# A two-layer expert kernel: the first expert's output product with weights stationary for the two-tile chunks

## The chip, the cores and the metric

The kernel runs on one core of a Trainium2 chip. The metric is the device time of one execution in microseconds (us). The core has a matrix engine (TensorE, PE in the profile; its loads of the stationary operand are the separate row PEld), a vector engine (DVE), an activation engine (ACT), GpSimd (POOL) and a queue that issues DMAs (SyncE, SP). Each engine executes its own instructions in the order in which the program lists them and waits on semaphores for the others. Matrix products accumulate in PSUM banks of 512 fp32 numbers for each of 128 partitions; ACT copies them to SBUF, from where DMAs go to DRAM.

## What is computed

Attention with a top-32 mask over 4 batches, 8 heads, 576 positions and head size 64; its output, as 2304 tokens of 512 numbers, goes through a gated expert (512 to 1536 to 512) and then through a second expert with a cosine (512 to 2048 to 512). All in fp32.

```python
scores = q @ k.T / 8
mask   = scores >= (32nd largest of the row)
attn   = softmax(where(mask, scores, -1e9))
x  = (attn @ v) as [2304, 512]
g  = x @ w_gate
x1 = (g * sigmoid(g) * (x @ w_val)) @ w_out      # first expert
h  = x1 @ w_in
out = (h * cos(h)) @ w2_out                      # second expert
```

## The kernel before

The 2304 tokens are 18 tiles of 128. They are worked on in ten chunks: two chunks of one tile (chunks 0 and 1, "turned" and in plain fp32) and eight chunks of two tiles, 256 tokens (chunks 2 to 9). In the two-tile chunks each fp32 operand is split into a high and a low fp32r part, and a product is three matmuls: high with high, low with high, high with low.

A chunk goes through these stages. Attention: for each of 4 head pairs, each tile and each head a "unit" (144 in all): scores on PE (`unit_proc`, line 586 plain in chunks 0 to 2, line 593 in split parts later), a copy by ACT (line 598), four maxima and three strikes on DVE (lines 623 and 626), the exponential on ACT, transposes of the result (line 687), the product with v (lines 740 and 743), and the normalised output x (the last step is line 824 on POOL). First expert: for each of 12 slices f of the hidden size the gate and value products (`gemm_proc`, line 899; gv, in the last chunk gvl), the activation, and a high and a low part gh and gl of the result (lines 958 and 962); then the output product (`wout_proc`, line 1063), accumulated over the 12 slices in two PSUM banks y0 and y1. The slice's weights wo (512 KB, high and low) come by DMA into a ring of two buffers. Second expert: `h_proc` (line 1279) and `o_proc` (line 1344); its input is read back from DRAM, transposed, as [feature, token] (`x2_proc`).

In `wout_proc` a two-tile chunk has the tokens as stationary operand: for each slice and each of the two tiles three matmuls with a 128x128 block of gh or gl stationary and 512 columns of wo moving (line 1063). So bank y0 holds 128 tokens x 512 features, y1 the next 128 tokens. The second expert wants features on the partitions, so `y_proc` turns each bank: for each half of it a copy to SBUF by ACT (line 1096, tile yo), two transposes on PE back into the bank (line 1102), a second copy by ACT (line 1107) and a DMA to DRAM (line 1108). There is one yo buffer (`r_yo`, a ring of 1), so a half starts when the DMA of the half ahead of it is done. A bank is free for the next chunk (`r_y`) after its second half.

The order of the instructions is made ahead of time, in Python, by `Plan`: every step is a generator that yields an engine, an estimated cost, a function that issues the instructions, and a due time. `Plan.run` picks, of the steps that are ready by these estimates on the engine that is free first, the one that is due earliest. The chip then executes the lists as they are. Each step of an output product is due 5 us after the gate and value product of the same slice (`moe_due`), and these are spread evenly over the time of one chunk's attention. A change of one cost can therefore change the order anywhere behind it.

Of the kernel before, what the change touches and what calls it, by code (L numbers as in the profile page):

```python
# [9 lines left out]
F32 = mybir.dt.float32  # L10
# [6 lines left out]
AF = mybir.ActivationFunctionType  # L17
# [36 lines left out]
RAWC = 3  # L54
SC_LEAD = 14.0
# [106 lines left out]
def topk_attention_moe_moe(ctx: ExitStack, tc: tile.TileContext, qT, kT, vP, w1, wo1, w2, out):  # L162
    nc = tc.nc
    plan = Plan()
# [3 lines left out]
    y1 = dram.tile([128, KT, NTOK], F32, name="y1")  # L168
# [12 lines left out]
    pools = {}  # L181

    def opened(name, **kw):
        pools[name] = tc.alloc_tile_pool(name=name, bufs=1, **kw)
        return pools[name]

    moe = opened("moe")
# [5 lines left out]
    psG = opened("psG", space=PSUM)  # L193
    gvt = [psG.tile([128, DM], F32, name=f"gv{g}") for g in range(2)]
    yt = [psL.tile([128, DM], F32, tag=f"y{i}", name=f"y{i}") for i in range(NYB)]
    sc = psR.tile([128, 2, 512], F32, name="sc")

    nc.scalar.activation(halfpi, halfpi, AF.Copy)
# [21 lines left out]
    r_pre, r_wo = Ring(6), Ring(2)  # L220
# [27 lines left out]
    W1X, W1, WO = {}, {}, {}  # L248
# [4 lines left out]
    ev_wo = {(c, f): Event() for c in range(NCH) for f in range(NF1)}  # L253
# [53 lines left out]
    def wo_index(c, f):  # L307
        return c * NF1 + f
# [247 lines left out]
    r_x, r_rs = Ring(NX), Ring(1)  # L556
# [9 lines left out]
    def unit_proc(u):  # L566
        c, p, t, h = units[u]
        segs = segments(FIRST[c] + t)
        due = due_unit(u)
        st = {}  # L570
        g = group[c, t]
        t0, n = ATT[c][g]
# [25 lines left out]
            nc.scalar.activation(st["s"], sc[:, :, :HALF], AF.Copy)  # L598

        yield r_sc.gate(u)  # L600
        end = yield "PE", 0.575 * len(segs) if c >= RAWC else 0.98, qk, due - SC_LEAD, True
        if h and (c, t) == (RAWC - 1, SIZES[c] - 1):
            r_k.free(1 + p, end, plan)
        for b, r0, r1 in segs:
# [4 lines left out]
        end = yield "ACT", 0.53, copy, due - SC_LEAD + 1.0, True  # L609
# [9 lines left out]
        for i in range(TOPK // 8):  # L619
# [9 lines left out]
            end = yield "DVE", 0.675, best, due, True  # L629
# [9 lines left out]
        end = yield "POOL", 0.175, bounds, due, True  # L639
# [16 lines left out]
        end = yield "ACT", 0.68, keep, due + 6.0, True  # L656
# [11 lines left out]
        end = yield "ACT", 0.77, expo, due + 9.0, True  # L668
# [173 lines left out]
    NG0 = KT // 2  # L842
    G0 = [sum((NF1 // 2 - NG0) // 2 if turned else NF1 for turned in TURNED[:c]) for c in range(NCH)]
    for i in range(G0[PLAIN]):
        r_g.freed[i] = Event(2)
    GV0 = [sum(NF1 // 4 if turned else NF1 for turned in TURNED[:c]) for c in range(NCH)]
    ev_y1 = [Event() for _ in range(NTOK // 128)]
    yo_count = [0]

    def moe_due(c, f):  # L850
        return due_unit((FIRST[c] + SIZES[c]) * H) + 20.0 + f * SIZES[c] * H * PACE / NF1
# [194 lines left out]
        for j in range(2):  # L1046
            ev_g[c, 2 * fp + j].set(end, plan)

    def wout_proc(c):
        turned = TURNED[c]  # L1050
        for f in range(NF1):
            k = c * NF1 + f
            yield ev_g[c, f]
            yield ev_wo[c, f]

            def part(t, f=f, k=k):
                bank = yt[(FIRST[c] + t) % NYB]
                cs = slice(t * 128, t * 128 + 128)
                g = G[c, f // 2][:, f % 2] if turned else None
                terms = ((g, WO[k]),) if turned else [(G[c, f][m][:, cs], WO[k][:, a])  # L1060
                                                      for m, a in ((0, 0), (1, 0), (0, 1))]
                for n, (m, w) in enumerate(terms):
                    nc.tensor.matmul(bank, m, w, start=f == 0 and n == 0, stop=f == NF1 - 1 and n == len(terms) - 1)  # L1063

            for t in range(SIZES[c]):
                i = FIRST[c] + t
                if f == 0:
                    yield r_y[i % NYB].gate(i // NYB)
                end = yield "PE", 0.93 if turned else 0.7, lambda t=t, part=part: part(t), moe_due(c, f) + 5.0, False
                if f == NF1 - 1:  # L1070
                    plan.start(y_proc(c, i), end)
            if not turned:
                r_g.free(G0[c] + f, end, plan)
            elif f % 2 and f // 2 >= NG0:
                r_g.free(G0[c] + (f // 2 - NG0) // 2, end, plan)
            if c:
                r_wo.free(wo_index(c, f), end, plan)
            else:
                wo0_free(f, end)
        if turned:  # L1080
            r_x.free(2 + c, end, plan)

    def y_proc(c, i):
        due = moe_due(c, NF1)
        bank = yt[i % NYB]
        y4 = bank.rearrange("p (f n) -> p f n", f=KT)
        for half in range(2):
            ko = yo_count[0]
            yo_count[0] += 1
            yield r_yo.gate(ko)  # L1090
            y2 = y4[:, 2 * half:2 * half + 2]
            st = {}

            def fetch(y2=y2):
                st["y"] = moe.tile([128, 2, 128], F32, tag="yo", name="yo", bufs=r_yo.n)
                nc.scalar.activation(st["y"], y2, AF.Copy)

            yield "ACT", 0.27, fetch, due, True

            def turn(y2=y2):  # L1100
                for j in range(2):
                    nc.tensor.transpose(y2[:, j], st["y"][:, j], ident)

            yield "PE", 0.22, turn, due + 2.0, True

            def store(y2=y2, half=half):
                nc.scalar.activation(st["y"], y2, AF.Copy)
                nc.sync.dma_start(y1[:, 2 * half:2 * half + 2, i * 128:i * 128 + 128], st["y"])

            end = yield "ACT", 0.27, store, due, True  # L1110
            r_yo.free(ko, end + 2.5, plan)
        r_y[i % NYB].free(i // NYB, end, plan)
        ev_y1[i].set(end + 2.5, plan)


    O_LAG = 12.0
# [1 line left out]
    ev_pb, ev_pbx, ev_ph, ev_pbo = Event(), Event(), Event(), Event()  # L1118
# [100 lines left out]
    def x2_proc(j):  # L1219
        yield ev_pb  # L1220
        pb = pools["pb"]
        for i in range(j * TPB, (j + 1) * TPB):
            yield ev_y1[i]
        due = b_due(j, 0) - (25.0 if j else 75.0)
        st = {}
        yield r_x2s.gate(j)

        def hi(k):
            if k == 0:
                X2[j] = [pb.tile([128, KT, CB], F32R, tag=f"x2{a}", name=f"x2{a}", bufs=r_x2s.n) for a in "hl"]  # L1230
            nc.scalar.activation(X2[j][0][:, k], st["x"], AF.Copy)  # L1231

        def load(k):
            st["x"] = pb.tile([128, CB], F32, tag="x2", name="x2", bufs=r_x2.n)
            nc.sync.dma_start(st["x"], y1[:, k, j * CB:j * CB + CB])

        for k in range(KT):
            yield r_x2.gate(j * KT + k)
            yield "DMA", 1.0, lambda k=k: load(k), due, True
            yield "ACT", 0.41, lambda k=k: hi(k), due, True  # L1240
            end = yield ("POOL", 0.95,
                         lambda k=k: nc.gpsimd.tensor_sub(X2[j][1][:, k], st["x"], X2[j][0][:, k]), due, True)  # L1242
            r_x2.free(j * KT + k, end, plan)
        ev_x2[j].set(end, plan)
# [3 lines left out]
    def h_proc(j, f):  # L1248
        k = j * NF2 + f
        due = b_due(j, f)  # L1250
# [4 lines left out]
        if k < H_ONE:  # L1255
            second, third, i = False, k % 3 == 2, k // 3 if k % 3 == 2 else k // 3 * 2 + k % 3
        else:
            second, third, i = k % 2, False, (k - H_ONE) // 2 if k % 2 else H_ONE * 2 // 3 + (k - H_ONE) // 2
        rh = r_hb if second else r_hc if third else r_h
        if second:  # L1260
            yield r_y[i % 2].gate(NTOK // 128 // NYB)
        elif not third:
            yield ev_ph
        yield rh.gate(i)
        pb = pools["pb"]
        st = {}
# [15 lines left out]
        for kk in range(KT):  # L1282
            end = yield "PE", 0.526, lambda kk=kk: part(kk), due, False
# [13 lines left out]
        def rest():  # L1297
# [5 lines left out]
        end = yield ("DVE", 0.46, lambda: nc.vector.scalar_tensor_tensor(r, st["k"], -C2, r, op0=OP.mult,  # L1303
                                                                        op1=OP.add), due, True)
# [10 lines left out]
        end = yield "DVE", 0.46, prod, due, True  # L1315
# [11 lines left out]
        end = yield "DVE", 0.46, lambda: nc.vector.tensor_sub(GT[j, f][1], st["g"], GT[j, f][0]), due, True  # L1327
# [64 lines left out]
    for c in range(NCH):  # L1392
        for f in range(NF1):
            if c:
                plan.start(wo_proc(c, f))
            if not TURNED[c]:
                plan.start(gemm_proc(c, f))
            elif f % 2:
                plan.start(turned_gemm_proc(c, f // 2))
        plan.start(wout_proc(c))  # L1400
    plan.start(pool_b_proc())
    plan.start(pool_h_proc())
    plan.start(pool_c_proc())
# [48 lines left out]
```

## Time and profile before

| | us |
|---|---|
| median of three runs | 1257.34 |
| lowest and highest of them | 1255.83, 1258.74 |
| the profiled execution | 1255.94 |
| its span, first to last instruction | 1253.9 |
| PE busy | 1200.3 |
| PEld busy | 1043.6 |
| DVE busy | 975.1 |
| ACT busy | 923.8 |
| POOL busy | 632.0 |

The span is the time from the first to the last instruction in one profiled execution; some 2 us lie around it. Attention and the first expert fill the span up to about 860 us, side by side; behind that there is the second expert alone. PE's busy time counts each matmul with its latency, and overlapping ones once, so the pace of matmuls is read from the starts of neighbours in a timeline, not from their durations.

### The profile page before, as it was taken

How to read it: one execution, taken by the hardware profiler on the slowest of the kernel's cores; microseconds unless marked ns; L12 is line 12 of the kernel's file. 1: busy time of each engine (PE TensorE's matmuls, PEld its weight loads, DVE VectorE, ACT ScalarE, POOL GpSimd, SP SyncE). 2: the span in 40 equal slices, each digit the busy share in tenths (PEclk: the TensorE clock that was granted, in tenths of full speed). 3: DMA queues.
4: the chain of work that ended last, by engine and by line, in shares of the span. 5: the costliest groups of instructions: out<-in, count | busy, mean ns of one | idle time of the engine just before them, and what ended most of it. 6: DMA issues, size and time to landing. Idle time of an engine off the chain costs nothing.

```text
span 1253.9 us, 22487 instructions
## 1 busy us (share of the span) xinstructions
PE 1200.3 (96%) x7528; PEld 1043.6 (83%) x7528; DVE 975.1 (78%) x1938; ACT 923.8 (74%) x2081; POOL 632.0 (50%) x1082
## 2 busy tenths in 40 slices
PE   6799889999999999999999999999999999999998
PEld 3577657898888898988898988897999989898997
DVE  6999999999999999998999993447555555555553
ACT  4789999899888888888898876557565656565554
POOL 4898976776777776877776755533010101010000
PEclk9799989999999999999999999999999999999999
DMA  7555556665656655556555332871010101010000
GB/s 253 159 175 168 179 163 201 206 211 168 194 164 180 190 170 175 181 162 203 181 160 189 124 116 85 268 261 39 1 51 1 51 1 51 1 38 1 18 8 26
DMA packets 88547, 162.14 MB, mean 129 GB/s; under 512 B 17008, under 2 KB 44144, under 8 KB 88432
## 3 DMA queue, kind: packets, MB, share of 16 engines
q1 hardware_dynamic: 88272, 160.65, 40.4%
q8 instruction: 59, 0.97, 0.3%
q14 instruction: 56, 0.46, 0.1%
q10 hardware_dynamic: 160, 0.07, 0.0%
HBM read 133.41 MB, written 27.26 MB: 128 GB/s over the span
## 4 chain that ended last, share of the span: by engine, by line
PE 58%; DMA 8%; ACT 6%; POOL 3%; DVE 2%; issue 2%; SPq 0%; POOLq 0%; ACTq 0%
PE o L1344 16%; PE h L1279 15%; PE gv L899 10%; PE y L1063 7%; PE av L743 2%; PE sc L593 2%; DMA wo<-wo 2%; DMA kx<-in_kT 2%; PE tp L687 2%; PE gvl L899 2%; DMA y<-yo 1%; DMA w_raw<-in_w 1%; DMA qx<-in_qT 1%; ACT e L654 1%; POOL K L496 1%
## 5 line engine op out<-in xcount | busy, mean ns | idle before, releaser
L623 DVE MAX8 m<-w 128x8 f32<-128x576 f32 x432 | 311.0, 747 | 1.8
L899 PE MATMUL gv<-x,w 128*128 128x256 f32 x2016 | 283.7, 288 | 1.7 <-ACT hg L866 1.6
L899 PEld LDWEIGHTS gv<-x,w 128*128 128x128 f32 x2016 | 259.0, 190 | 8.6 <-ACT hg L866 2.8
L1279 PE MATMUL h<-x2h,w 128*128 128x384 f32 x768 | 214.5, 338 | 0.0
L626 DVE MATCH_REPLACE8 w<-m,w 128x576 f32<-128x576 f32 x288 | 213.3, 742 | 0.0
L1344 PE MATMUL o<-w,gh 128*128 128x512 f32 x576 | 195.8, 395 | 0.0
L1242 POOL TENSOR_TENSOR x2l<-x,x2h 128x384 fp32r<-128x384 f32 x24 | 25.8, 1075 | 262.1 <-ACT x2h L1231 262.1
L1063 PE MATMUL y<-wo,gh 128*128 128x512 f32 x400 | 148.5, 413 | 6.7 <-DMA wo<-wo 5.1
L1313 DVE TENSOR_TENSOR g<-r,h 128x384 f32<-128x384 f32 x96 | 53.1, 554 | 118.5 <-ACT r L1308 118.5
L1279 PEld LDWEIGHTS h<-x2h,w 128*128 128x128 f32 x768 | 140.6, 188 | 4.3
L1279 PE MATMUL h<-x2l,w 128*128 128x384 f32 x384 | 129.3, 337 | 0.0
L1306 ACT ACTIVATE r<-r 128x384 f32<-128x384 f32 x96 | 50.4, 525 | 103.9 <-DVE r L1303 103.9
L1344 PEld LDWEIGHTS o<-w,gh 128*128 128x128 f32 x576 | 108.1, 188 | 21.0
L654 ACT ACTIVATE e<-s,b 128x576 f32<-128x576 f32 x144 | 114.2, 794 | 8.2 <-POOL b L637 8.1
L623 DVE MAX8 m<-s 128x8 f32<-128x576 f32 x144 | 107.7, 748 | 15.9 <-ACT s L598 14.5
L665 ACT ACTIVATE e<-e,b 128x576 f32<-128x576 f32 x144 | 114.2, 793 | 2.8 <-POOL b L641 0.3
L1344 PE MATMUL o<-w,gl 128*128 128x512 f32 x288 | 113.6, 394 | 1.0 <-DVE gl L1327 1.0
L598 ACT ACTIVATE s<-sc 128x576 f32<-128x576 f32 x144 | 95.4, 662 | 21.6 <-PE sc L586 16.2
L626 DVE MATCH_REPLACE8 w<-m,s 128x576 f32<-128x576 f32 x144 | 106.9, 742 | 0.0
L693 ACT ACTIVATE pt<-tp 128x512 f32<-128x512 f32 (+1 forms) x216 | 101.9, 503 | 4.9 <-PE tp L687 3.3
L687 PE MATMUL tp<-ident,e 128*128 128x128 f32 x648 | 99.4, 277 | 5.9 <-ACT pt L693 3.3
L1327 DVE TENSOR_TENSOR gl<-g,gh 128x384 fp32r<-128x384 f32 x96 | 56.4, 588 | 58.0 <-ACT gh L1324 58.0
(106 smaller groups left out, 2489.6 us busy)
## 6 DMA issues: line engine op xcount, KB each, us to landing
wo<-wo SPq DMA_DIRECT2D x96, 512.0 KB, 3.7
w_raw<-in_w SPq DMA_DIRECT2D x32, 511.8 KB, 4.3
V<-in_vP SPq DMA_DIRECT2D x52, 256.0 KB, 3.0
w<-in_w SPq DMA_DIRECT2D x24, 511.5 KB, 5.5
kx<-in_kT SPq DMA_DIRECT2D x64, 144.0 KB, 3.1
wo<-wo SPq DMA_DIRECT2D x36, 256.0 KB, 2.9
w2d<-w_raw SPq DMA_DIRECT2D x32, 256.0 KB, 2.6
cvx<-w2d SPq DMA_DIRECT2D x32, 256.0 KB, 4.5
```

The costliest lines, as they stand in the source:

```text
L598: nc.scalar.activation(st["s"], sc[:, :, :HALF], AF.Copy)
L623: nc.vector.max(out=st["m"][:, 8 * i:8 * i + 8], in_=st["w"] if i else st["s"])
L626: nc.vector.match_replace(out=st["w"], in_to_replace=st["m"][:, 8 * i:8 * i + 8], in_values=st["w"] if i else st["s"], imm_value=LOWEST)
L654: nc.scalar.activation(st["e"], st["s"], AF.Prelu, bias=st["b"][:, 1:2], scale=SCALE, alpha=STEEP)
L665: nc.scalar.activation(st["e"], st["e"], AF.Exp, bias=st["b"][:, 2:3], scale=1.0, accum_out=smT[c, p, g][:, j:j + 1])
L687: nc.tensor.transpose(st["ps"][:, j - j0], e[:, j * 128:j * 128 + 128], ident)
L693: nc.scalar.activation(pt[:, j0:j1], st["ps"][:, :j1 - j0], AF.Copy)
L899: nc.tensor.matmul(gv[g], W1[f, kk // 2][:, a, g, kk % 2], m, start=kk == 0 and i == 0, stop=kk == KT - 1 and i == 2)
L1063: nc.tensor.matmul(bank, m, w, start=f == 0 and n == 0, stop=f == NF1 - 1 and n == len(terms) - 1)
L1279: nc.tensor.matmul(st["h"], w[:, a, kk * 128:kk * 128 + 128], m[:, kk], start=kk == 0 and n == 0, stop=kk == KT - 1 and n == 2)
L1327: end = yield "DVE", 0.46, lambda: nc.vector.tensor_sub(GT[j, f][1], st["g"], GT[j, f][0]), due, True
L1344: nc.tensor.matmul(o[t], a[:, cs], W2[f, 1][:, m], start=f == 0 and n == 0, stop=f == NF2 - 1 and n == 2)
```

## The change

For the eight two-tile chunks the operands of the output product change places. For each slice and each of four blocks d of 128 features, three matmuls have a 128x128 block of wo stationary (high, high, low) and 256 tokens of gh, gl and gh moving: 12 matmuls of 256 columns for each slice, where there were 6 of 512. Bank y0 then holds feature blocks 0 and 1, y1 blocks 2 and 3, each with features on the partitions and 256 tokens along the row. So nothing is transposed: each of the four blocks is copied once by ACT and stored by DMA. The turned one-tile chunks keep the old way, in a function of their own.

The steps on PE are four for each slice, with an estimated cost of 0.38 each, instead of two with 0.7. Bank y0 is free after the copy of block 1, y1 after that of block 3; the product of the next chunk asks for y0 ahead of block 0 and for y1 ahead of block 2. The copies still go through the one yo buffer, but those of chunk 8 (`late`) wait until the attention's memory is given back and then use four buffers of their own. The events of stored tiles become events of stored chunks. In `unit_proc` the estimated cost of a unit's scores goes from 0.98 to 1.25 in the plain chunks, and from 0.575 to 0.58 for each segment in the others.

```diff
+    y1p = [x.rearrange("p (a b) -> p a b", a=2) for x in yt]
...
-        end = yield "PE", 0.575 * len(segs) if c >= RAWC else 0.98, qk, due - SC_LEAD, True
+        end = yield "PE", 0.58 * len(segs) if c >= RAWC else 1.25, qk, due - SC_LEAD, True
...
+    def bank_turn(c, b):
+        return c // 2 if c < PLAIN else c - PLAIN + (PLAIN + 1 - b) // 2
...
-                terms = ((g, WO[k]),) if turned else [(G[c, f][m][:, cs], WO[k][:, a])
-                                                      for m, a in ((0, 0), (1, 0), (0, 1))]
-                for n, (m, w) in enumerate(terms):
-                    nc.tensor.matmul(bank, m, w, start=f == 0 and n == 0, stop=f == NF1 - 1 and n == len(terms) - 1)
...
-                end = yield "PE", 0.93 if turned else 0.7, lambda t=t, part=part: part(t), moe_due(c, f) + 5.0, False
-                if f == NF1 - 1:
-                    plan.start(y_proc(c, i), end)
...
+    def wout_proc(c):
+        t0 = FIRST[c] * 128
+        for f in range(NF1):
+            k = c * NF1 + f
+            due = moe_due(c, f) + 5.0
+            yield ev_g[c, f]
+            yield ev_wo[c, f]
+
+            def part(d, f=f, k=k):
+                w = WO[k]
+                gh, gl = G[c, f]
+                for i, (a, m) in enumerate(((0, gh), (0, gl), (1, gh))):
+                    nc.tensor.matmul(y1p[d // 2][:, d % 2], w[:, a, d * 128:d * 128 + 128], m,
+                                     start=f == 0 and i == 0 and d % 2 == 0, stop=f == NF1 - 1 and i == 2,
+                                     skip_group_check=True)
+
+            for d in range(KT):
+                if f == 0 and d % 2 == 0:
+                    yield r_y[d // 2].gate(bank_turn(c, d // 2))
+                end = yield "PE", 0.38, lambda d=d, part=part: part(d), due, False
+            r_g.free(G0[c] + f, end, plan)
+            r_wo.free(wo_index(c, f), end, plan)
+        due = moe_due(c, NF1)
+        late = c == NCH - 2
+        if late:
+            yield ev_pb
+        for d in range(KT):
+            if not late:
+                yield r_yo.gate(yo_count[0])
+
+            def fetch(d=d):
+                if late:
+                    y = pools["pb"].tile([128, CH], F32, tag=f"yo{d}", name="yo")
+                else:
+                    y = moe.tile([128, CH], F32, tag="yo", name="yo", bufs=r_yo.n)
+                nc.scalar.activation(y, y1p[d // 2][:, d % 2], AF.Copy)
+                nc.sync.dma_start(y1[:, d, t0:t0 + CH], y)
+
+            end = yield "ACT", 0.27, fetch, due, d == 0
+            if not late:
+                r_yo.free(yo_count[0], end + 2.5, plan)
+                yo_count[0] += 1
+            if d % 2:
+                r_y[d // 2].free(bank_turn(c, d // 2), end, plan)
+        ev_y1[c].set(end + 2.5, plan)
...
-        for i in range(j * TPB, (j + 1) * TPB):
-            yield ev_y1[i]
+        for c in range(NCH):
+            if FIRST[c] < (j + 1) * TPB and FIRST[c] + SIZES[c] > j * TPB:
+                yield ev_y1[c]
```

## Rows read from the trace of the kernel before

**Rows 1.** The page's first part: each engine's busy time, share, instructions.
```profile
PE 1200.3 (96%) x7528; PEld 1043.6 (83%) x7528; DVE 975.1 (78%) x1938; ACT 923.8 (74%) x2081; POOL 632.0 (50%) x1082
```
**Rows 2.** Busy time by stretch: PE, PEld, DVE, ACT, POOL (instructions); clock, DMA share.
```profile
0.00:100.00 100.00, 76.97 (x374) 55.49 (x374) 89.64 (x194) 70.83 (x154) 75.86 (x148) 0.93 0.60 191
...
200.00:763.00 563.00, 551.62 (x4157) 493.85 (x4158) 546.40 (x1126) 489.78 (x1192) 404.32 (x748) 1.00 0.55 174
763.00:786.00 23.00, 23.00 (x168) 19.62 (x167) 0.18 (x1) 12.06 (x32) 13.06 (x23) 1.00 0.28 90
786.00:852.00 66.00, 61.86 (x418) 57.11 (x417) 32.78 (x51) 37.51 (x80) 34.54 (x29) 1.00 0.76 252
852.00:880.00 28.00, 26.55 (x135) 23.42 (x134) 18.99 (x30) 17.98 (x38) 6.37 (x5) 1.00 0.12 34
```
**Rows 3.** PE's groups by shape: count, busy us, mean ns; idle before, releasers.
```profile
L899 PE MATMUL gv<-x,w 128*128 128x256 f32 x2016 | 283.7, 288 | 1.7 <-ACT hg L866 1.6
...
L1063 PE MATMUL y<-wo,gh 128*128 128x512 f32 x400 | 148.5, 413 | 6.7 <-DMA wo<-wo 5.1 <-ACT yo L1107 0.6 <-POOL wo L244 0.5
...
L1102 PE MATMUL y<-ident,yo 128*128 128x128 f32 x72 | 15.0, 290 | 3.2 <-ACT yo L1096 2.9
```
**Rows 4.** Timeline of PE at a chunk's end: start, us, what [idle before].
```profile
293.18 0.40 PE L1063 MATMUL y<-wo,gh 128*128 128x512 f32 x1
...
294.57 0.52 PE L899 MATMUL gv<-x,w 128*128 128x256 f32 x3
...
299.73 0.44 PE L1102 MATMUL y<-ident,yo 128*128 128x128 f32 x2 [0.39 <-ACT yo L1096]
299.92 0.95 PE L899 MATMUL gv<-x,w 128*128 128x256 f32 x6
...
307.18 0.50 PE L1063 MATMUL y<-wo,gh 128*128 128x512 f32 x1
307.52 0.40 PE L1063 MATMUL y<-wo,gl 128*128 128x512 f32 x1
...
313.67 3.03 PE L899 MATMUL gv<-x,w 128*128 128x256 f32 x24
```
**Rows 5.** PE's waits, 200 to 763 us: total us, times, longest.
```profile
PE y L1063 <- DMA wo<-wo: 2.5, 5, 1.0
PE y L1102 <- ACT yo L1096: 1.7, 3, 1.0
```
**Rows 6.** DVE's first maxima, 200 to 763 us: busy, mean ns, idle before.
```profile
L623 DVE MAX8 m<-s 128x8 f32<-128x576 f32 x108 | 80.8, 748 | 7.2 <-ACT s L598 5.8 <-POOL th L951 1.2
```
**Rows 7.** Timeline of ACT at the same chunk's end: copies of the banks.
```profile
294.08 0.38 ACT L1096 ACTIVATE yo<-y 128x256 f32<-128x256 f32 x1
...
300.71 0.39 ACT L1107 ACTIVATE yo<-y 128x256 f32<-128x256 f32 x1
...
310.91 0.54 ACT L1107 ACTIVATE yo<-y 128x256 f32<-128x256 f32 x1
```
**Rows 8.** The page's DMA issues: count, KB each, median us to landing.
```profile
y<-yo SPq DMA_DIRECT2D x36, 128.0 KB, 2.0
```
**Rows 9.** Timeline of POOL: the last part of the last chunk's x.
```profile
784.46 0.74 POOL L824 TENSOR_TENSOR x<-rs,x 128x256 fp32r<-128x256 f32 x1 [0.53 <-ACT x L820]
```
**Rows 10.** Timeline of PE from there: last chunk's first products.
```profile
785.91 5.20 PE L899 MATMUL gvl<-x,w 128*128 128x256 f32 x42
...
802.04 0.49 PE L1063 MATMUL y<-wo,gh 128*128 128x512 f32 x1
...
813.01 0.47 PE L1063 MATMUL y<-wo,gh 128*128 128x512 f32 x1 [1.69 <-DMA wo<-wo]
```
**Rows 11.** Timeline of PE at the start: the first unit's plain scores.
```profile
5.26 2.26 PE L586 MATMUL sc<-kr,qr 128*128 128x288 f32 x4 [5.26 <-DMA kr<-in_kT]
```

More of the change, by code (lines that the diff above doesn't have):

```diff
@@ L846, in topk_attention_moe_moe @@
     GV0 = [sum(NF1 // 4 if turned else NF1 for turned in TURNED[:c]) for c in range(NCH)]
-    ev_y1 = [Event() for _ in range(NTOK // 128)]
+    ev_y1 = [Event() for _ in range(NCH)]
     yo_count = [0]
@@ L1047, in turned_gemm_proc, with turned_wout_proc, part @@
             ev_g[c, 2 * fp + j].set(end, plan)
-    def wout_proc(c):
-        turned = TURNED[c]
+    def bank_turn(c, b):
+        return c // 2 if c < PLAIN else c - PLAIN + (PLAIN + 1 - b) // 2
+    def turned_wout_proc(c):
+        bank, b = yt[c % NYB], c % NYB
+        yield r_y[b].gate(bank_turn(c, b))
         for f in range(NF1):
-            k = c * NF1 + f
             yield ev_g[c, f]
             yield ev_wo[c, f]
[L1056 to L1059, printed above, removed]
-                terms = ((g, WO[k]),) if turned else [(G[c, f][m][:, cs], WO[k][:, a])
-                                                      for m, a in ((0, 0), (1, 0), (0, 1))]
-                for n, (m, w) in enumerate(terms):
-                    nc.tensor.matmul(bank, m, w, start=f == 0 and n == 0, stop=f == NF1 - 1 and n == len(terms) - 1)
[L1065 to L1068, printed above, removed]
-                end = yield "PE", 0.93 if turned else 0.7, lambda t=t, part=part: part(t), moe_due(c, f) + 5.0, False
-                if f == NF1 - 1:
-                    plan.start(y_proc(c, i), end)
-            if not turned:
-                r_g.free(G0[c] + f, end, plan)
-            elif f % 2 and f // 2 >= NG0:
+            def part(f=f):
+                nc.tensor.matmul(bank, G[c, f // 2][:, f % 2], WO[c * NF1 + f], start=f == 0, stop=f == NF1 - 1)
+            end = yield "PE", 0.93, part, moe_due(c, f) + 5.0, False
+            if f % 2 and f // 2 >= NG0:
                 r_g.free(G0[c] + (f // 2 - NG0) // 2, end, plan)
@@ L1079, in wout_proc @@
                 wo0_free(f, end)
-        if turned:
-            r_x.free(2 + c, end, plan)
-    def y_proc(c, i):
+        r_x.free(2 + c, end, plan)
         due = moe_due(c, NF1)
-        bank = yt[i % NYB]
         y4 = bank.rearrange("p (f n) -> p f n", f=KT)
         for half in range(2):
-            ko = yo_count[0]
-            yo_count[0] += 1
-            yield r_yo.gate(ko)
+            yield r_yo.gate(yo_count[0])
             y2 = y4[:, 2 * half:2 * half + 2]
@@ L1107, in store @@
                 nc.scalar.activation(st["y"], y2, AF.Copy)
-                nc.sync.dma_start(y1[:, 2 * half:2 * half + 2, i * 128:i * 128 + 128], st["y"])
+                nc.sync.dma_start(y1[:, 2 * half:2 * half + 2, FIRST[c] * 128:FIRST[c] * 128 + 128], st["y"])
             end = yield "ACT", 0.27, store, due, True
-            r_yo.free(ko, end + 2.5, plan)
-        r_y[i % NYB].free(i // NYB, end, plan)
-        ev_y1[i].set(end + 2.5, plan)
+            r_yo.free(yo_count[0], end + 2.5, plan)
@@ new lines, in turned_wout_proc @@
+            yo_count[0] += 1
+        r_y[b].free(bank_turn(c, b), end, plan)
+        ev_y1[c].set(end + 2.5, plan)
[25 more added lines that the diff above has]
+            if not late:
+                yield r_yo.gate(yo_count[0])
+            def fetch(d=d):
[7 more added lines that the diff above has]
+            if not late:
+                r_yo.free(yo_count[0], end + 2.5, plan)
+                yo_count[0] += 1
+            if d % 2:
+                r_y[d // 2].free(bank_turn(c, d // 2), end, plan)
+        ev_y1[c].set(end + 2.5, plan)
@@ L1260, in h_proc @@
         if second:
-            yield r_y[i % 2].gate(NTOK // 128 // NYB)
+            yield r_y[i % 2].gate(bank_turn(NCH, i % 2))
         elif not third:
@@ L1399, in topk_attention_moe_moe @@
                 plan.start(turned_gemm_proc(c, f // 2))
-        plan.start(wout_proc(c))
+        plan.start((turned_wout_proc if TURNED[c] else wout_proc)(c))
     plan.start(pool_b_proc())
```

## The prediction, made before the changed kernel ran

> **What bounds the kernel now.** I read the page's busy times first, then the table by stretch, then the groups and waits of the engines that are full. PE is busy for 96% of the span [rows 1], but not evenly: in the first 100 us it stands idle for 23.0 us, from 200 to 763 us for 563 - 551.6 = 11.4 us, then not at all to 786 us, and for 4.1 and 1.5 us in the two stretches to 880 us [rows 2]. The reader is to see in the same table that DVE is nearly as full from 200 to 763 us, 546.4 of 563 us, with 16.6 us idle: PE and DVE share that stretch, and PE's work is not clearly its only limit. What DVE waits for there by name is mostly the scores' copy, 5.8 us [rows 6]. The second thing to see is how the chunks join. The last part of the last chunk's x is done at 784.46 + 0.74 = 785.2 us, and its first products start at 785.91 us [rows 9, 10]. So the first expert is not far behind attention: it takes each x as it comes. PE work that is removed ahead of 763 us helps only as far as it lets attention go faster too. PE's clock is full from 200 us on [rows 2], so no term below has a slower one.
>
> **The matmuls.** In the timeline six of 512 columns take 294.57 - 293.18 = 1.39 us [rows 4]. The new shape, 128x128 stationary and 256 columns moving in fp32r, is that of the gate and value products, which also reload one operand of three: 24 of them take 3.03 us with the last one's duration of 0.288 us in it [rows 3, 4], so (3.03 - 0.288) / 23 = 0.119 us from start to start. Twelve are 1.43 us, 0.04 more for each slice, and 8 x 12 = 96 slices make **+4 us**. The columns are 3072 for a slice either way, so below 0 it does not go. The upper bound is the pace just behind a transpose, where six take 0.95 us: (0.95 - 0.288) / 5 = 0.132, or 1.59 for a slice and +19 us. I stay at +4, since the run of 24 is nearest to a run of 12.
>
> What the row shows of this price can be weighed against a rule. The Trainium skill ("TensorE: Matmul & The Clock Gate", section "Back-to-back issue gap") gives a gap of N/2.4 + 2.5 ns for matmuls at the full clock, an estimated 109 ns at 256 columns and 216 at 512. By it the term would be 96 x (12 x 0.109 - 6 x 0.216) = +1.2 us in place of +4. Here the rows show 0.119 and 0.232 us, slower than the rule in both shapes, so I keep the rows; by the rule the sum below would gain some 1.8 us more.
>
> **The transposes.** The 72 transposes are 36 pairs, of which the one-tile chunks keep 4; 32 pairs go. A pair takes 299.92 - 299.73 = 0.19 us, and the six products behind it take 0.07 us more than at their pace (0.95 - 0.288 - 5 x 0.119) [rows 4]: 0.26 x 32 = 8.3 us. The 0.07 may fall on another neighbour once the pair is gone; without it the lower end is 0.19 x 32 = 6.1 us. The upper end is the group's busy time, in which each pair's latency counts whole: 15.0 / 36 x 32 = 13.3 us [rows 3]. Near to the timeline, I take **-7.5 us**. Ahead of the transposes PE sits idle for 3.2 us in all, 2.9 of it for the copy [rows 3]: 32/36 of that is **-2.8 us**. A wait that goes can come back as one for the next late operand, and on this engine that is the weights wo, 2.5 us from 200 to 763 us [rows 5]; so this part is worth between 0 and -2.8. PE's own sum is 4 - 7.5 - 2.8 = -6.3 us.
>
> **What of it reaches the end.** Chunks 2 to 7, three quarters of all this (-4.7), lie ahead of 763 us, beside a DVE that is 97% busy. DVE's 16.6 idle us are the most that attention could gain, and 5.8 of them are tied to scores that PE and ACT deliver. I let half of the -4.7 through, **-2.4 us**, with 0 and -4.7 as ends. Chunks 8 and 9 lie behind the last scores, where PE alone is full: **-1.6 us** whole.
>
> **The copies and the banks.** For each chunk ACT copied eight times 128x256 and now copies four times. At 0.38 to 0.54 us a copy [rows 7] that frees some 32 x 0.4 = 13 us of ACT, which is no limit (489.8 of 563 us busy [rows 2]). It can make scores' copies earlier; the bound is the 5.8 us of rows 6, and I take **-0.5 us**. The first copy of a chunk's banks starts at 294.08 us, bank y0 is free at 300.71 + 0.39 = 301.1, y1 at 311.45 [rows 7]. The new copies still share one buffer, so each waits for the DMA of the one before, 2.0 us from issue to landing [rows 8], some 2.8 us a step with the copy and the issue: y0 is free after about 3.5 us instead of 7, y1 after about 9 instead of 17. What is queued behind a waiting copy on ACT is the scores' copy and the exponentials, and DVE waits for them, but four waits a chunk stay four. On SP the same 32 stores wait for ACT, with wo and other loads queued behind; nothing is moved past another queue in the code. In chunk 8 the copies have four buffers and follow one another. There the last chunk's gate products started at 785.91 us, but its output product only at 802.04, and at 813.01 it stood 1.69 us for wo, whose two buffers had been held until then [rows 10]. I take **-1.0 us** of the 5.6 us idle from 786 to 880 us; the ends are 0 and -5.6. The wait for the attention's memory costs nothing where x of chunk 9 is ready (785.2 us) ahead of the last product of chunk 8; if that ran 5 us sooner, the copies would wait up to 5 us, with the last output product behind them.
>
> **Finer steps.** Each slice is now four steps of 0.38 that the plan may place apart, instead of two of 0.7. A run of output products that follows other work pays 307.52 - 307.18 = 0.34 us in place of 0.23 for its first interval [rows 4], 0.11 us a break. About ten breaks more give **+1.0 us**.
>
> **The plain scores' cost.** It executes nothing; it tells the plan that 32 units take 0.27 us longer. A unit's four matmuls really take 2.26 us at the start [rows 11], so the plan comes nearer to the chip. DVE is idle for 100 - 89.6 = 10.4 us of the first 100 [rows 2], and 7.5 of these pass before the first scores are done [rows 11]: at most 2.9 us to gain, and by the same size to lose. I take 0.
>
> **Sum:** -2.4 - 1.6 - 0.5 - 1.0 + 1.0 = -4.5 us. The profiled execution took 1255.9 us with a span of 1253.9; it would take 1251.4 with 1249.4. It lies 1.4 us under the median of the runs, from which the forecast is 1257.3 - 4.5 = **1252.8 us**.
>
> **Rivals.** (1) *Attention paces the rest.* DVE is full to 763 us, so PE's saving there turns into idle time of PE, and the handover through one buffer is no sooner than the plan can use. What stays is -1.6 us and the +1.0: about 1256.7. For it speaks the x that arrives just as it is used; against it, that PE is 98% busy and that scores do make DVE wait. (2) *The finer steps are split*, the case on the other side. Now the products of a slice mostly stand in one run. If half of the 384 steps stood alone, that would be 192 more breaks of 0.11 us, 21 us; weighed like the saving (half of it ahead of 763 us) 0.625 x 21 = 13 us, against a sum of -5.5 without the breaks: 1264.8. It decides from 80 more breaks, where the sum is 0. Against it speaks that the steps of one slice become ready together and have one due time, and that in the rows six products mostly stand together; for it, that each end of a step is a place where a due transpose or score comes first. A mild form, 100 to 120 breaks, gives 1258.7 to 1260.1. (3) *All of it comes through:* -6.3 on PE, the 4 us of wo and copies between 786 and 880 us, -0.5: 1246.5. (4) *The banks do not come free sooner*, so the handover does not do what it says: then the -1.0 is lost and the time is 1253.8, within the forecast's own range.
>
> **How the numbers follow.** A measurement of this kernel can tell about 0.2%, 2.5 us, from no change. The forecast with (4) has 0.45, range 1249 to 1254.8; (3) has 0.13; (1) has 0.24; (2) has 0.18. Faster is 0.45 + 0.13 = 0.58, same 0.24, slower 0.18. The range that should hold 8 in 10 goes from a little below (3), 1245.5, to the mild form of (2), 1260.5; it takes in the 2.9 us either way of the plan's new cost. The severe form of (2) and a sum beyond (3) are left out.
>
> **What will show it.** In the changed profile the output product's groups should have 1152 matmuls of 256 columns, 0.12 us from start to start, in runs of 12; the transposes of y should be 8; ACT's copies of banks 32 fewer. PE's idle time from 200 to 763 us tells (1) from the forecast: if it rises from 11.4 to 15 us or more while DVE stays at 97%, attention paces. Runs of 3 or 6 in the output product would show (2). The last chunk's output product should start less than 12 us behind its first gate product, not 16. The forecast is wrong if the last x comes later than 785 us: then the new order of the plan, and not these terms, has set the time.

## The result: slower, by an order of the steps that had no term

| | before | after |
|---|---|---|
| median, us | 1256.59 (6 runs) | 1262.78 (6 runs) |
| the profiled execution's span, us | 1253.9 | 1260.0 |
| ratio, 95% interval | | 1.0064 (1.0040 to 1.0087) |

The forecast was 1252.8 us with a range of 1245.5 to 1260.5; the changed kernel is 6.2 us slower than before by the medians (1.0049) and 8 us by the ratio; the interval holds both. The busy times by stretch, with the columns of [rows 2]:

```profile
200.00:763.00 563.00, 545.68 (x4543) 510.37 (x4541) 543.71 (x1117) 482.72 (x1159) 402.82 (x743) 1.00 0.54 173
763.00:786.00 23.00, 22.98 (x191) 20.95 (x191) 3.59 (x8) 12.04 (x32) 12.76 (x22) 1.00 0.28 93
786.00:852.00 66.00, 62.46 (x500) 61.49 (x496) 27.40 (x47) 33.28 (x72) 32.78 (x30) 1.00 0.76 252
852.00:880.00 28.00, 24.58 (x112) 22.30 (x113) 20.60 (x30) 17.70 (x38) 10.42 (x7) 0.88 0.13 43
```

From 200 to 763 us PE is idle for 17.3 us, where it was 11.4 [rows 2]; at the end of the first expert, 852 to 880 us, for 3.4 instead of 1.5, and its mean granted clock is 0.88 there. The work itself came out as costed. PE's groups by shape (columns of [rows 3]), the first product groups of the last chunk in PE's timeline, and the last part of the last x in POOL's:

```profile
L1112 PE MATMUL y<-gh,wo 128*128 128x256 f32 x768 | 158.4, 288 | 8.4 <-DMA wo<-wo 3.5 <-ACT yo L1135 2.7 <-ACT hg L867 1.5
L1112 PE MATMUL y<-gl,wo 128*128 128x256 f32 x384 | 110.8, 288 | 2.8 <-DVE gl L963 1.6 <-POOL gl L963 0.6
L1086 PE MATMUL y<-ident,yo 128*128 128x128 f32 x8 | 1.6, 285 | 0.6 <-ACT yo L1080 0.6
```

```profile
789.62 5.20 PE L900 MATMUL gvl<-x,w 128*128 128x256 f32 x42
794.65 0.28 PE L1112 MATMUL y<-gh,wo 128*128 128x256 f32 x1
...
796.10 0.88 PE L900 MATMUL gvl<-x,w 128*128 128x256 f32 x6
796.82 0.28 PE L1112 MATMUL y<-gh,wo 128*128 128x256 f32 x1
```

```profile
788.12 0.74 POOL L825 TENSOR_TENSOR x<-rs,x 128x256 fp32r<-128x256 f32 x1 [0.53 <-ACT x L821]
```

There are 1152 matmuls of 256 columns; a slice's twelve take 796.10 - 794.65 = 1.45 us, against the 1.43 of the forecast; 8 transposes of y are left; of the 96 runs of the two-tile chunks' output products 84 are of exactly 12, six of 6 and six of 18 (93 runs before). The last chunk's output product starts at 796.82 us, 7.2 us behind its first gate product, where it was 16.1 [rows 10]: the banks do come free sooner. But the last part of x ends at 788.86 us, 3.7 us later than before [rows 9], and that is the sign that the prediction named for a time set by the new order of the plan.

### The profile page after: what moved, and what is told of

Same layout as the page of the kernel before. It is cut to its first block, busy times and chain, and to the rows that moved or that the text cites. A ratio compares the mean times of both kernels' runs of the same rounds, so it can differ in the third digit from the quotient of the medians.

```text
span 1260.0 us, 23395 instructions
## 1 busy us (share of the span) xinstructions
PE 1198.4 (95%) x8040; PEld 1071.0 (85%) x8040; DVE 979.4 (78%) x1938; ACT 916.8 (73%) x2049; POOL 633.2 (50%) x1082
## 4 chain that ended last, share of the span: by engine, by line
PE 45%; DVE 18%; ACT 12%; DMA 10%; POOL 8%; issue 5%; SPq 1%; POOLq 0%; ACTq 0%; DVEq 0%
PE o L1376 16%; PE h L1311 16%; DVE m L624 9%; DVE w L627 8%; PE y L1112 4%; PE gv L900 3%; POOL K L497 2%; DMA w_raw<-in_w 2%; DMA qx<-in_qT 2%; DMA kx<-in_kT 2%; PE gvl L900 2%; ACT e L666 2%; PE av L744 2%; ACT e L655 1%; ACT s L599 1%
## 5 line engine op out<-in xcount | busy, mean ns | idle before, releaser
L900 PEld LDWEIGHTS gv<-x,w 128*128 128x128 f32 x2016 | 255.1, 191 | 7.5 <-ACT hg L867 5.2
L1112 PE MATMUL y<-gh,wo 128*128 128x256 f32 x768 | 158.4, 288 | 8.4 <-DMA wo<-wo 3.5
L1112 PEld LDWEIGHTS y<-gh,wo 128*128 128x128 f32 x768 | 126.5, 191 | 16.6 <-issue 6.2
L655 ACT ACTIVATE e<-s,b 128x576 f32<-128x576 f32 x144 | 113.0, 785 | 12.7 <-POOL b L638 12.6
L1112 PE MATMUL y<-gl,wo 128*128 128x256 f32 x384 | 110.8, 288 | 2.8 <-DVE gl L963 1.6
L599 ACT ACTIVATE s<-sc 128x576 f32<-128x576 f32 x144 | 94.7, 658 | 18.7 <-PE sc L587 15.7
```

The costliest lines, as they stand in the source:

```text
L655: nc.scalar.activation(st["e"], st["s"], AF.Prelu, bias=st["b"][:, 1:2], scale=SCALE, alpha=STEEP)
L900: nc.tensor.matmul(gv[g], W1[f, kk // 2][:, a, g, kk % 2], m, start=kk == 0 and i == 0, stop=kk == KT - 1 and i == 2)
L1112: nc.tensor.matmul(y1p[d // 2][:, d % 2], w[:, a, d * 128:d * 128 + 128], m, start=f == 0 and i == 0 and d % 2 == 0, stop=f == NF1 - 1 and ...
```

## The experiments

Three theories were open. **W**: the new work costs more than its terms. **O** and **S**: the work is as costed, and the order in which the plan lists the steps, which changes with any planned cost, is what costs (O: a cause in this change; S: any remade order). **P**: attention paces all that lies ahead of 763 us, so that PE's savings do not arrive. The order is made from the planned costs alone and does not look at the instructions that a step issues. So an edit inside a step's function keeps the order of everything else, and an edit of a cost keeps the work and remakes the order. The traces bear this out: in e1, e2, e3 and e9 the compute instructions outside the output product, its transposes and its copies (6832 on PE, 2009 on ACT, 1938 on DVE, 1082 on POOL) come in the order of the kernel before, while in e4 PE's order differs from the 74th of them on, at 38.6 us. All ratios are to runs of the kernel before on the same chip.

**The work in the old order.** In e1 each matmul is cut in two, in e2 the turning is left out, e3 has both:

```diff
+                    for q in range(2):       # e1, e3
+                        nc.tensor.matmul(bank[:, q * 256:q * 256 + 256], m, w[:, q * 256:q * 256 + 256], ...)
...
-                for j in range(2):           # e2, e3; the first copy (L1096) likewise
+                for j in range(2 if TURNED[c] else 0):
                     nc.tensor.transpose(y2[:, j], st["y"][:, j], ident)
```

> The kernel before, its order of all steps kept; only each 512-column matmul of the two-tile chunks' output product is cut into two of 256 columns (1152 matmuls, 12 a slice, as in the change). If the work itself is what was mis-sized (theory W), this alone costs +5 us or more. If my term holds it costs +4 us on PE, of which 0.625 arrives: +2.5 us. If the new order of the steps is the cause (theory O), between 0 and +4 us, and the slowdown of the change lies elsewhere.

> The kernel before in its own order, with the turning left out for the two-tile chunks: no transposes of y (64 fewer) and one ACT copy of each half bank instead of two (32 fewer); the first expert's output is stored unturned. My terms: -7.5 - 2.8 = -10.3 us on PE, 0.625 of it at the end: -6.4 us. If attention's DVE paces everything ahead of 763 us (theory P): -2.6 us. Theory W, under which the transposes stood beside idle time: 0.

> Both edits together: the work of the changed kernel in the order of the kernel before (256-column matmuls, no transposes, one copy of each half bank; the output of the first expert is stored unturned). Theory O: faster than before, some -4 us, and then the 6 us by which the change is slower come from the order of its steps, about 10 us of them. Theory W: slower than before by some 6 us. Theory P: 0 to -1 us.

e1: 1.0039 (1.0025 to 1.0053), +4.9 us. e2: 0.9962 (0.9945 to 0.9978), -4.8 us. e3: 0.9959 (0.9941 to 0.9977), -5.1 us. The finer matmuls cost what they should on PE, and nothing of it is hidden; the work as a whole gains. W is out by e3, for which it asked for +6. P asked for 0 to -1 in e3, outside the interval, and for -2.6 in e2, just outside of it. The two terms do not add up (4.9 - 4.8 is not -5.1): why the cut costs nothing once the transposes are gone was not found. In the single profiled executions they nearly do, up to a fixed point of the program (+4.2 - 6.0 against -3.1, below).

**Costs alone.** e4 takes over only the new costs of the scores, e6 and e7 one of the two, and e5 takes them out of the changed kernel:

```diff
-        end = yield "PE", 0.575 * len(segs) if c >= RAWC else 0.98, qk, due - SC_LEAD, True
+        end = yield "PE", 0.58 * len(segs) if c >= RAWC else 1.25, qk, due - SC_LEAD, True
```

> The kernel before with only the planned costs of the scores changed (1.25 for plain ones, 0.58 a segment for the others). No instruction is added or removed, only the order differs. My step took 0 with 2.9 us either way. Theory O lets it be any of -6 to +6 us; if it is +4 us or more, this part of the change alone carries the slowdown. Theories W and P: 0.

> The changed kernel with the planned costs of the scores put back (0.98 and 0.575). If the two parts add up, it is 7.8 us faster than the changed kernel: some 1255, within 2 us of the kernel before; if the weight-stationary product brings what its work brought in the old order (-5.8 us), 1249.5. If any change of the order costs by itself (theory S, a shuffle), it is slow too, 1259 or more.

> The kernel before with the planned cost of the plain scores alone at 1.25. If the longer plain scores are the cause (theory L: the plan orders everything behind them by times that the chip does not have), +7.8 us, with DVE waiting some 4 us more for copied scores behind 200 us. If the 0.58 or the mix is the cause: 0 to +2 us.

> The kernel before with the planned cost of the split scores alone at 0.58 a segment. Theory L: 0, within 2 us. Theory S, by which a change of any cost moves the time by several us: anything from -4 to +8 us, with no relation to its size (0.005 us a segment).

e4: 1.0063 (1.0042 to 1.0084), +7.9 us with no instruction of work added or removed, as much as the whole change. e6: 1.0013 (0.9996 to 1.0031). e7: 1.0017 (0.9997 to 1.0037). e5: 1.0036 (1.0020 to 1.0052), so in the changed kernel the new scores' costs make 3.5 us of the loss (1.0064 / 1.0036), known only within some 3.5 us. Neither half of the edit carries the loss by itself, and without the edit the changed kernel is still slower than before, by 4.5 us, although its work gains 5. So the scores' cost is not *the* cause (theory L falls), and the question became whether any new order costs.

**Controls.** e8 and e12 change nothing that the change touches, only the planned cost of the old output product's step, from 0.70 to 0.71 and to 0.69.

> A control that is no part of the change: the kernel before with the planned cost of an output product step at 0.71 instead of 0.70; no instruction is added or removed. Theory L: 0, within 2 us. Theory S: a difference of 3 us or more to either side, since the order is remade from the first such step on.

> A second control that is no part of the change: the kernel before with 0.69 instead of 0.70 as the planned cost of an output product step. Theory S: slower than the kernel before by 1 to 8 us, as the four other orders of the same work were (+1.6, +2.1, +6.9 and +7.8 us): its own order is the lucky one. If a lower cost is as good as a higher one is bad: faster.

e8: 1.0055 (1.0034 to 1.0077), 6.9 us for 0.01 in a cost. e12: 1.0005 (0.9988 to 1.0022). Here are two stretches of e8 and then one of e4, as above:

```profile
200.00:763.00 563.00, 543.73 (x4106) 487.04 (x4105) 540.26 (x1113) 484.30 (x1178) 399.15 (x739) 1.00 0.55 172
...
852.00:880.00 28.00, 24.16 (x123) 20.41 (x122) 21.03 (x30) 21.30 (x46) 13.20 (x9) 1.00 0.19 59
```

```profile
200.00:763.00 563.00, 544.25 (x4101) 486.27 (x4100) 540.99 (x1112) 485.89 (x1177) 398.88 (x737) 1.00 0.56 172
```

PE stands idle for 19.3 and 18.8 us in the long stretch, more still than the 17.3 of the changed kernel. The lower clock of the changed kernel at the end of the first expert is not the common cause: from 852 to 880 us it is 1.00 in e8 (above) and in e4. S holds in its main point: with the old work a remade order costs 0 to 8 us, with no relation to the size or the sign of the edit. Its stronger form, that every other order is clearly slower, falls with e12.

**The change in the old order.** e9 is the deciding run: the whole weight-stationary product, its result stored as the second expert needs it, but under the steps, costs and due times of the kernel before.

```diff
+                for d in (2 * t, 2 * t + 1):          # the old step of tile t, cost 0.7
+                    for i, (a, m) in enumerate(((0, gh), (0, gl), (1, gh))):
+                        nc.tensor.matmul(y1p[t][:, d % 2], w[:, a, d * 128:d * 128 + 128], m, ...)
...
+                    nc.scalar.activation(y, y1p[t][:, half], AF.Copy)      # the old step "store"
+                    nc.sync.dma_start(y1[:, 2 * t + half, FIRST[c] * 128:FIRST[c] * 128 + CH], y)
```

> The whole weight-stationary product of the change (wo stationary, 12 matmuls of 256 columns, one copy and one store of each feature block, no transposes of y), but with the steps, costs and due times of the kernel before, so that everything else stands in its order. Order theories (O, S): as the work measured alone in that order, 1249 to 1252 against 1255 to 1258 of the kernel before, -4 to -6 us, and 12 us under the changed kernel. If weights stationary itself costs on the chip (theory W): +4 us or more.

e9: 1251.3 us, 0.9961 (0.9946 to 0.9976), -4.9 us. The same work is 11.5 us apart in the two orders by the medians, 13 us by the ratios. Its stretches, and where its last chunk starts:

```profile
200.00:763.00 563.00, 551.07 (x4589) 516.74 (x4589) 543.17 (x1120) 485.54 (x1169) 403.13 (x748) 1.00 0.55 174
763.00:786.00 23.00, 23.00 (x192) 21.43 (x189) 0.18 (x1) 10.13 (x27) 13.11 (x21) 1.00 0.34 116
786.00:852.00 66.00, 61.86 (x479) 60.27 (x479) 37.15 (x56) 38.15 (x81) 38.30 (x30) 1.00 0.72 241
852.00:880.00 28.00, 28.00 (x143) 25.46 (x142) 16.97 (x31) 15.72 (x32) 2.39 (x2) 1.00 0.09 29
```

```profile
783.42 5.20 PE L900 MATMUL gvl<-x,w 128*128 128x256 f32 x42
```

PE is idle for 11.9 us in the long stretch, as in the kernel before, and the last chunk starts 2.5 us earlier than before [rows 10] and 6.2 us earlier than in the changed kernel.

**Forms of the step.** e10 has 0.36 for 0.38 in the changed kernel, e11 two steps of 0.7 for each slice instead of four.

> The changed kernel with the planned cost of an output product step at 0.36 (what it takes on the chip) instead of 0.38. Theory S: another order, and the time may be anything from 1250 to 1266, with no relation to the better cost. If the plan was misled by a cost that is too high: faster than the changed kernel by 3 us or more.

> The changed kernel with two steps of 0.7 for each slice, one for each bank, instead of four of 0.38; the rest as changed. My rival 2 (finer steps are split and cost a break each): faster than the changed kernel by 3 us or more, with longer runs of the output product. Theory S: any time from 1250 to 1266, since the order is another one again.

e10: 1.0009 (0.9991 to 1.0027); e11: 1.0013 (0.9997 to 1.0029); by the ratios 6.9 and 6.4 us faster than the changed kernel, and still slower than e9 by 6 us. For e11 that is what rival 2 asked for, but not by its mechanism: it has 82 runs of 12 where the changed kernel has 84. Both read as draws of another order.

**What in an order costs.** One place in the changed kernel shows how a late step travels. Timelines of SP, ACT, PE and DVE (start, us, what, idle before):

```profile
552.40 5.37 SPq L1136 DMA_DIRECT2D y<-yo  x2
557.81 0.91 SPq L538 DMA_DIRECT2D V<-in_vP  x1
...
560.04 1.28 SPq L511 DMA_DIRECT2D qx<-in_qT  x2
```

```profile
565.16 0.42 ACT L520 ACTIVATE q<-qx 128x256 fp32r<-128x256 f32 x1 [2.96 <-DMA qx<-in_qT]
```

```profile
566.11 0.33 PE L688 MATMUL tp<-ident,e 128*128 128x128 f32 x1 [1.54 <-ACT pt L694]
...
569.98 1.23 PE L594 MATMUL sc<-K,q 128*128 128x288 f32 x8
```

```profile
571.92 0.76 DVE L624 MAX8 m<-s 128x8 f32<-128x576 f32 x1 [3.46 <-ACT s L599]
```

SP stands 4.7 us for a copy of the bank before it can issue the second of the two stores, and the q load queued behind is issued at 560.04 us. ACT, with copies for PE queued behind, stands 2.96 us for it, PE 1.54 us for ACT, the scores come late and DVE stands 3.46 us. Each engine works through its list in order, so here one load that is late by the plan's clock stops three engines. Three handles on this were tried in the changed kernel, the first also in e9:

```diff
-                nc.sync.dma_start(y1[:, d, t0:t0 + CH], y)       # e13; e16 the same in e9
+                nc.scalar.dma_start(y1[:, d, t0:t0 + CH], y)
...
-SC_LEAD = 14.0                                                   # e14
+SC_LEAD = 18.0
...
-    LAT = {..., "DMA": 2.0, ...}                                 # e15
+    LAT = {..., "DMA": 3.0, ...}
```

> The changed kernel, same order of every engine, with the stores of the two-tile chunks' output product issued by ACT behind its copy instead of by SP, so that loads queued behind them on SP (q, k, v, wo) no longer stand for ACT's copy. If these held loads make the scores late (theory Q: in one place of the changed kernel's trace SP stands 4.7 us ahead of such a store, the q load behind it comes late, ACT stands 3.0 us for it and DVE 3.5 us for the scores): 2 to 5 us faster than the changed kernel, with DVE's wait for copied scores behind 180 us down from 10.5 to 6 us. If lateness has many other sources: within 2 us of it.

> The weight-stationary product in the order of the kernel before, with its stores issued by ACT instead of SP. Theory Q: 1 to 3 us faster than with SP's stores (0.3961% under the kernel before), since SP stood 24.5 us for these copies there too. Otherwise within 2 us of it, or slower by what 32 issues cost on ACT.

> The changed kernel with the scores of each unit due 18 us ahead of its maxima in the plan instead of 14. If late scores are what the new order costs (theory D): DVE's wait for copied scores falls below 6 us and the time by 3 us or more. If the order is merely another one with no such handle (theory S): any time from 1251 to 1266, and the wait and the time need not go together.

> The changed kernel with 3.0 instead of 2.0 us for a DMA's landing in the plan, nearer to the 3.0 to 4.3 us from issue to landing of the q, k, v and weight loads in the traces. If ACT standing for loads that the plan takes for landed is the source (21.5 us behind 180 us in the changed kernel, 17.2 in the kernel before): these waits fall under 15 us and the time by 3 us or more. Theory S: any time from 1251 to 1266.

e13: 1.0133 (1.0104 to 1.0162); e16: 1.0022 (1.0003 to 1.0042). The stores on ACT cost 8.6 us against the changed kernel (1.0133 / 1.0064) and 7.7 against e9 (1.0022 / 0.9961). With the stores off SP, ACT's wait for q behind 180 us fell from 7.6 to 4.3 us, but DVE's for copied scores did not (10.5 and 10.7 us), which theory Q asked for. So held stores are not shown to be what slows the new orders; the time that the issues take on ACT (below) may hide a gain. e14: 1.0054 (1.0035 to 1.0073). DVE's waits for copied scores from 200 to 763 us (us, times, longest), first in the changed kernel, then in e14:

```profile
DVE m L624 <- ACT s L599: 9.5, 9, 3.5
```

```profile
DVE m L624 <- ACT s L599: 2.8, 5, 1.1
```

The wait went, and the time did not: PE is still idle for 16.3 us in that stretch (546.70 of 563 busy), and for 4.1 us from 852 to 880 us. Part of the wait came back elsewhere: DVE's wait for POOL (sm, L771) rose from 3.4 to 6.6 us. This wait of DVE is no handle on the time. e15: 0.9996 (0.9979 to 1.0014), 8.5 us faster than the changed kernel by the ratios, but the waits that it was to cut stand as they were: ACT's for loads and stores from 180 to 763 us are 19.8 us in all, 21.5 in the changed kernel and under 15 by the expectation. So this too is not shown to be more than another order.

**Chunk 8's handover.** e17 adds the four buffers (`late`) alone to e9, e18 takes them from the changed kernel (`late = False`).

> The weight-stationary product in the order of the kernel before, with the change's own four buffers for chunk 8's copies, which wait until the attention's memory is given back. The order is the old one up to the end of chunk 8's output product (788 us), so only the chunk's handover behind it can differ. My term for this handover: -1.0 us, between 0 and -5.6; theory S, which lets even this part of the order cost: 0 to +4 us.

> The changed kernel with chunk 8's copies through the one buffer like the others; its order is kept up to the end of chunk 8's output product. In the traces the kernels with the change's four-step form take 105 to 110 us from the last chunk's first gate product to a fixed point of the second expert, the new work in the old order 103 us. If the four buffers are what costs there: 3 to 5 us faster than the changed kernel. If they help as I costed: 1 us slower or more.

e17: 0.9962 (0.9949 to 0.9975), the same as e9 (0.9961). e18: 1.0040 (1.0025 to 1.0055), 3 us under the changed kernel by the two ratios, with intervals that overlap. In the old order nothing of my -1.0 for the handover is to be seen, although the last chunk's output product starts 9.0 us behind its first gate product in e17 and 15.1 us in e9; 1 us is less than the two runs can tell (some 2.5 us). In the new order it may cost.

**All orders side by side**, by ratio, with PE's idle time from 200 to 763 us:

| work | order | ratio | PE idle, us |
|---|---|---|---|
| old | before | 1 | 11.4 |
| old | e12, e6, e7 | 1.0005, 1.0013, 1.0017 | 12.8, 15.5, 13.5 |
| old | e8, e4 | 1.0055, 1.0063 | 19.3, 18.8 |
| new | old order: e9, e17 | 0.9961, 0.9962 | 11.9, 12.6 |
| new | e15, e10, e11 | 0.9996, 1.0009, 1.0013 | 15.7, 16.5, 16.2 |
| new | e5, e18, e14, changed kernel | 1.0036, 1.0040, 1.0054, 1.0064 | 14.2, 15.5, 16.3, 17.3 |

None of the twelve remade orders is faster than the old order with the same work (e18 is the changed kernel's own order up to some 797 us). The three nearest with the old work (e12, e6, e7) cannot be told from it; with the new work all seven are slower than e9, by 4.4 to 13 us. That fits an order that was found by trying many costs, but how it was found is not to be seen in any run.

## Why the prediction was wrong, step by step

**The step that failed** is the price of a remade order: the prediction had none. For the plan's new cost it says "It executes nothing ... I take 0", with 2.9 us either way, and e4 measured +7.9 for the costs alone. The bound was worked out from DVE's idle time in the first 100 us, as if a cost of the first 32 units could move only these. In e4 the first maxima of the 33rd unit come 1.0 us later than before (177.7 against 176.7), and those of the last unit 6.5 us later (763.2 against 756.7): 5.5 us of the loss come behind the stretch that I looked at, as the order behind it is remade. The reading beside it was thin as well: the 2.26 us of [rows 11] hold for the first seven of the 32 plain units, but 21 of them take 1.13 to 1.24 us, about as far from the old 0.98 as from the new 1.25. The same goes for **the finer steps**, costed at +1.0 us by breaks in the runs. The breaks did not come (96 runs for 93). That four steps in place of two make another order altogether had no term, and in the changed kernel this is the larger part: e5, with the old scores' costs, is 9.5 us slower than e9 (1.0036 / 0.9961). The rivals had the same hole. Each was a mechanism of the new work or of its pace; none was an order that is worse everywhere. The last sentence of the prediction names the new order as what would make it wrong, but gives it no size and no chance. The table of the kernel before has PE, DVE and ACT busy for 98, 97 and 87% of the long stretch [rows 2]; that this leaves little slack to take up a worse order is an argument, not shown by a run.

**The sum for the work** was -4.5 us with 0 for the plan, and e9 measured -4.9 (the +1.0 and the -1.0, for finer steps and handover, have no part in e9 and cancel). That the two agree is in part luck. By the median distances from start to start PE's work grows by 4 to 5 us with the finer matmuls (forecast +4) and shrinks by 7.0 with the 64 transposes at 0.109 us (forecast 7.5); the forecast added 2.8 us of waits and let 0.625 of it all through. In the profiled executions the time from PE's first matmul to the 145th of h is 886.4 us before, and 890.6, 880.4, 883.3 and 881.8 in e1, e2, e3 and e9: +4.2, -6.0, -3.1 and -4.6 us, where PE's work moved by 4 to 5, -7, and -2 to -3 in the last two. By the runs it is +4.9, -4.8, -5.1 and -4.9, each within some 2 us. Taken together this is nearer to the whole of PE's work than to 0.625 of it, but the share of a single term cannot be told so closely (e2's is 0.7), nor whether the waits gave anything: the 2 to 3 us of PE's work are about half of the -4.9, and where the rest comes from was not measured. In the changed kernel, with the work of e9, the same stretch takes 892.8 us, and in e4 and e8, with the work of before, 894.3 and 896.0.

**Rival 1** (attention paces the rest) had its sign, PE's idle time at 17.3 us with DVE at 543.7 of 563 us, and yet it was not the cause: e1 to e3 show PE's terms arriving. The sign was badly chosen, as e4 and e8 show the same with the old work. **Rival 2** is out by the runs of 12. **Rival 4** is out: in chunks 2 to 7 of the changed kernel y0 is free 3.0 to 4.1 us after the first copy and y1 9.7 to 11.1 (costed at 3.5 and 9), and in the kernel before 6.0 to 8.2 and 14.6 to 18.0. A gain from it is not to be seen: in e9, the faster kernel, y1 takes 13.1 to 16.2. What the prediction named as making it wrong, a last x later than 785 us, is what happened; but e1, in the old order, has it at 788.4 us too, so by itself this sign does not tell a new order from more work.

**The rule** of the Trainium skill ("TensorE: Matmul & The Clock Gate", section "Back-to-back issue gap") gives N/2.4 + 2.5 ns as the gap of a matmul by itself, and the prediction used it for a stream of them: an estimated 109 ns for each of 1152 matmuls of 256 columns, and +1.2 us for the term. The rows of the changed kernel show 0.12 us here too, and e1's +4.9 us (+3.1 to +6.7) agrees with the term from the rows and not with the rule's.

**Still open** is what property makes one order slow and another not. With the same work the idle time of PE goes with it only roughly (e5, at 14.2 us, is slower than e15 at 15.7), and neither the lead of the scores nor moving the stores changed it for the better.

## What to carry to other kernels

Where a program lists all its engines' work ahead of time from planned costs, an edit of a cost or of a step's grain is a change of the whole order behind it, and needs a term of its own; here its size was 0 to 8 us with the old work and 4 to 13 with the new. To measure what an edit is worth, put the new instructions into the old steps first, so that the order stays, and run one or two controls that remake the order with the old work. Then pick the order separately: the best version here is the new work in the old order, 1251.3 us.

## What the hardware showed beside this

Stores issued by ACT were dear in this kernel, where ACT is busy for 86% of the long stretch. The 32 of e13 took 0.33 us each on ACT's queue,

```profile
L1136 ACTq DMA_DIRECT2D y<-yo x32: 326/326/536, 301.3 to 881.2; - x32
```

(ns, least, median and most), 10.4 us in all, and the kernel became 8.6 us slower, 7.7 in the old order, although ACT counts only 476 and 483 of 563 us as busy in the two runs (e13 and e16): the issue is not in that busy time.

And in one place a lower clock came on top of a stop of PE. In the changed kernel PE stood 1.89 us for DVE at the start of the second expert's steady part; then the granted clock was at the lower of its two levels, 1.2 GHz, for a stretch:

```profile
862.55 0.45 PE L1311 MATMUL h<-x2h,w 128*128 128x384 f32 x1 [1.89 <-DVE g L1345]
...
864.22 0.52 PE L1311 MATMUL h<-x2l,w 128*128 128x384 f32 x1
864.54 0.84 PE L1311 MATMUL h<-x2h,w 128*128 128x384 f32 x2
```

```profile
863.50:866.70 3.20, 3.20 (x12) 3.01 (x11) 1.72 (x4) 1.92 (x5) 0.00 (x0) 0.50 0.12 41
```

Matmuls of 384 columns start 0.32 us apart there (864.54 - 864.22) instead of 0.175 and the clock's column says 0.50: about 1.6 us more for 3.2 us. That a stop of this length brings the lower clock is not shown: at 803.49 us of the same kernel PE had stood 2.92 us for wo, and the clock from 800 to 812 us is 1.00. In e9 PE is busy for all 28 us from 852 to 880 us, at the full clock.
